# A planned delta-rule and feed-forward kernel: another order of the work, weight decoding moved partly to ScalarE and TensorE, and key tiles of 128 rows

## The chip, the cores and the metric

The kernel runs on one core of one Trainium2 chip. The metric is the device time in microseconds (us); three runs of the kernel before gave 631.62 as their median, from 630.73 to 635.42.

## The reference

Two computations in a row. The first is a delta-rule recurrence for 4 batches x 8 heads over 768 time steps, with a 48 x 48 state per head; the second takes its result as 3072 tokens of 384 channels through a feed-forward layer with 2048 hidden units. The weights come as 64-bit floats.

```python
k_n = k / (np.linalg.norm(k, axis=-1, keepdims=True) + 1e-06)
for t in range(S):
    y[:, :, t] = q_t @ state
    v_old = state^T @ k_n_t
    state = state + beta_t * outer(k_n_t, v_t - v_old)
x = y as (3072, 384)
h = x @ w_in
g = h - np.tanh(h)
out = g @ w_out
```

## The kernel before

**The recurrence** is cut into 24 chunks of 32 steps, and six groups of four chunks. For each chunk `score` (L433) multiplies keys with keys and queries on TensorE, into a bank of PSUM; the key product goes to the group's tile `gs` (`L442` on VectorE for the first four chunks, `L445` on ScalarE for the others), the query product to `pq`, which GpSimd masks. For each group `solve` on VectorE inverts 128 triangular 32 x 32 matrices: a transpose (L476), norms (L485 to L516), a scaling (L519), 30 elimination steps of two instructions each (L530, L532), a second scaling and a transpose into `tt` (L535, L540). Then `chain` goes through the chunks one after the other, since each needs the state that the last one left: keys times state on TensorE (L576, `keyed`), the difference on VectorE (L583, `vsub`), `tt` times values (L608), a copy to SBUF on ScalarE (L614), the new outer products (L622), their addition to the state `st` on VectorE (L648), and the output's two products (L593, L632). `output` transposes a chunk's result (L667) and splits it in a high and a low part, the `xt` tiles (L671 on ScalarE, L673 on VectorE).

**The feed-forward layer** takes the tokens in six blocks of 512 (four chunks each). Every block has 16 units of 128 hidden channels: nine matmuls `ph` (L778), tanh on ScalarE (L795), a subtraction and a high/low split on both engines (L797, L803, L805), and nine matmuls `po` (L828). In the first block the first F0 = 5 units are worked in two halves of 256 tokens, so that they can start after two chunks.

**The weights** are decoded on the chip from the 64-bit words, in 16 pieces of 128 x 768: `c` from the high word on ScalarE (L690), `lo` from the low word on VectorE (L715), both joined on VectorE (L726), the high part `h` cast on ScalarE (L729), and the low part `l = c - h` on VectorE (L744). Each piece serves two units.

**What sets the order.** A planner in the kernel (`Plan.run`) picks the next operation of each engine at build time, from costs, due times and the constants at the end of the file; on the chip each engine then works through its fixed list and waits where a semaphore isn't there yet. While TensorE has nothing to do, the planner puts in padding matmuls on a zero tile (`warm`, L333). `FIRST` is the order of the first loads on SyncE's queue (SP); the weight pieces from AHEAD = 6 on are loaded from ScalarE's queue (`refill`). The tiles of keys and queries (`kc`, `kd`, L341) have KR = 112 rows of 2 x 512 numbers, the two batch pairs at rows 0 to 47 and 64 to 111.

Of the kernel before, what the change touches and what calls it, by code (L numbers as in the profile page):

```python
# [85 lines left out]
class Plan:  # L86
# [3 lines left out]
    SLACK = {"PE": 0.649, "DVE": 0.28, "ACT": 0.098, "POOL": 0.2, "SP": 0.0}  # L90
# [10 lines left out]

    def spawn(self, gen):
        op = next(gen, None)
        if op is not None:
            self.streams.append([gen, op])
# [86 lines left out]
    def run(self):  # L192
        nc, tc = self.nc, self.tc
        code = nc.cur_bb.bb.instructions
        while self.streams:
# [25 lines left out]
            try:  # L221
                item[1] = gen.send((t, end + self.VISIBLE[eng]))
# [24 lines left out]
def kernel(ctx: ExitStack, tc: tile.TileContext, kq, kn, vn, beta, w_in, w_out, const, out):  # L247
# [16 lines left out]
    cs = cst.tile([128, 160], F32, name="cs")  # L264
    ident = cs[:, 0:128]
    strict = cs[:, None, 128:160].broadcast_to([128, H, C])
# [22 lines left out]
    def transfer(end, kb):  # L289
        a = max(dma[0], end + 1.5)  # L290
        dma[0] = a + kb * 1024e-3 / 360.0
        plan.moves.append((a, dma[0]))
        return Event(dma[0] + 0.4)
# [19 lines left out]

    def negate():
        (_, t) = yield Op("ACT", 0.4, (const_in,), 10.0)
        nc.scalar.activation(minus, ident, AF.Copy, scale=-1.0)
        negation.t = t

    def warm():
# [3 lines left out]
        while xt_in[NS - 1].t is None and plan.free["PE"] < 2000.0:  # L323
# [5 lines left out]
            if 0 < len(gram) < 4:  # L329
# [9 lines left out]
    def load_keys(s, table, tag):  # L339
        kc = ld.tile([KR, 2, 16, C], F32, tag=tag, name=f"{tag}{s}", bufs={"kc": KCS, "kd": KDS}[tag])  # L340
# [6 lines left out]
    def load_values(s):  # L347
        v = ld.tile([128, H, D], F32, name="v", bufs=VS)
        nc.sync.dma_start(v, vn[s])
        a = transfer(plan.free["SP"], 192)  # L350
        kt = ld.tile([128, H, D], F32, name="kt", bufs=VS)
        nc.sync.dma_start(kt, kn[s])
        v_of[s] = (v, kt, a, transfer(plan.free["SP"], 192), rv.take())
# [33 lines left out]
    def loads(items):  # L387
        for item in items:
            kind, n = item[0], int(item[1:])
            deps, tag = (), "kd" if kind == "d" or n in (2, 3) else "kc"  # L390
# [6 lines left out]
            yield Op("SP", ISSUE * (2 if kind == "v" else 1), deps=deps, due=when(kind, n))  # L397
            if kind == "k":
                load_keys(n, kc_of, tag)
                if n in (2, 3):  # L400
# [12 lines left out]
    sol = lambda name: at.tile([128, C, C], F32, tag="sol", name=name, bufs=SOLS)  # L413
# [4 lines left out]
    def score(s):  # L418
        g, r = divmod(s, 4)
        deps = (known(kc_of, s, 1),)  # L420
        if r == 0:
            yield Op("PE", 0.0, deps + (rsol, lambda: 0.0 if g < 2 or g - 2 in solved else None), 0.0)
            gs = sol(f"gs{g}")
# [11 lines left out]
        if s not in (2, 3):  # L435
# [4 lines left out]
        if s < 4:  # L440
            (_, t) = yield Op("DVE", dve(256), (scored,), 0.0)
            nc.vector.tensor_copy(to, ps[:, :, 0:C])  # L442
# [17 lines left out]
    def solve(g):  # L460
# [9 lines left out]

        (_, t) = yield V(0, gram_done[g] + [known(beta_of, g, 1), rsol], cost=1.24)
        gs, gsr = groups[g]
        bt, _, btr = beta_of[g]
        a = sol(f"a{g}")
        ar = rsol.take()
        nc.vector.transpose(fl(a), fl(gs))  # L476
        gsr.t = t
# [10 lines left out]
        def triangle():  # L488
            (_, t) = yield Op("POOL", 1.27, (taken,), due(), "lock")
            nc.gpsimd.affine_select(a, a, [[1, C], [-1, C]], ALU.is_gt, 0.0, base=0, channel_multiplier=0)  # L490
# [27 lines left out]
        (_, t) = yield V(C * C, (scaled, tri), mode="lock")  # L518
        nc.vector.scalar_tensor_tensor(a, a, -1.0, gm[:, :, None].broadcast_to([128, C, C]), ALU.mult, ALU.mult)  # L519
# [4 lines left out]
        for j in range(1, C - 1):  # L524
            n = C - 1 - j
            shape = [128, n, j]
            (_, e) = yield V(n * j, (t,), mode="lock")
            tmp = at.tile([128, 240], F32, name="tmp", bufs=2)
            tv = tmp[:, :n * j].rearrange("p (i c) -> p i c", c=j)
            nc.vector.tensor_tensor(tv, a[:, j + 1:, j:j + 1].broadcast_to(shape), a[:, j:j + 1, :j].broadcast_to(shape), ALU.mult)  # L530
            (_, e) = yield V(n * j, (Event(e),), mode="lock")
            nc.vector.tensor_tensor(a[:, j + 1:, :j], a[:, j + 1:, :j], tv, ALU.add)  # L532
            t = Event(e)
        (_, e) = yield V(C * C, (t,), mode="lock")
# [425 lines left out]
```

## Time and profile before

| what | value |
|---|---|
| median of three runs | 631.62 us |
| the profiled execution's own time | 631.85 us |
| its span, first to last instruction | 630.1 us |
| what lies around the span | 1.75 us |
| TensorE busy | 596.3 us, 95% of the span |
| VectorE busy | 396.0 us, 63% |
| ScalarE busy | 203.1 us, 32% |
| GpSimd busy | 46.4 us, 7% |
| padding matmuls (L333) | 164, 46.1 us |
| mean granted TensorE clock | 0.967 |

In the rows of the profile each group has its line, engine, operation, tiles with their shapes, count, busy time and the mean of one; the timeline and the chain of waits give start and duration in us from the span's start; "<-" names what ended an idle time. PE is TensorE's matmuls, PEld its weight loads, DVE is VectorE, ACT ScalarE, POOL GpSimd, SPq and ACTq the DMA issues on SyncE's and ScalarE's queue. A small fp32 matmul has two records.

### The profile page before, as it was taken

To read this page: it belongs to the slowest core of one execution; us is meant where nothing else is said; L and a number is where in the kernel's file an instruction comes from. 1 tells how busy PE (TensorE), PEld (TensorE's weight loads), DVE (VectorE), ACT (ScalarE), POOL (GpSimd) and SP (SyncE) were. 2 spreads that over 40 slices of the span, in tenths; PEclk is the share of its full clock that TensorE was granted. 3 is DMA by queue.
4 is the path that set the end of the run, shared out by engine and by line. 5 is a ranking of instruction groups with operands and counts; after the bars stand their busy time and mean duration, and the time that the engine had idled before them with its cause. 6 is when DMAs were issued, how large, how long until landed. Compare 5 with 4: busy or idle time off the path is not lost.

```text
span 630.1 us, 24015 instructions
## 1 busy us (share of the span) xinstructions
PE 596.3 (95%) x11078; PEld 468.0 (74%) x11078; DVE 396.0 (63%) x853; ACT 203.1 (32%) x365; POOL 46.4 (7%) x60
## 2 busy tenths in 40 slices
PE   6769868999999999999999999999999999999996
PEld 3334547898888878888777888878888878878884
DVE  2859779998889659864278863289863333332331
ACT  2220204575434323224232224332232323332331
POOL 1200301001000010000110000110000000000000
PEclk8779975999999999999999999999999999999998
DMA  9990525361124032122222123022121000010001
GB/s 282 297 316 20 150 84 177 118 212 46 28 57 133 3 96 62 48 69 95 59 74 70 44 57 94 3 57 57 57 91 48 1 3 3 4 51 0 1 0 51
DMA packets 26789, 49.11 MB, mean 78 GB/s; under 512 B 2912, under 2 KB 9184, under 8 KB 26688
## 3 DMA queue, kind: packets, MB, share of 16 engines
q1 hardware_dynamic: 23184, 39.62, 21.2%
q10 hardware_dynamic: 3504, 7.95, 4.0%
q8 instruction: 87, 1.43, 1.0%
q14 instruction: 14, 0.11, 0.1%
HBM read 42.84 MB, written 4.72 MB: 75 GB/s over the span
## 4 chain that ended last, share of the span: by engine, by line
PE 85%; DMA 7%; DVE 5%; issue 1%; ACT 1%; SPq 0%; ACTq 0%
PE po L828 32%; PE ph L778 32%; DMA kc<-in_kq 5%; PE po L333 4%; PE psa L608 3%; PE psa L433 3%; PE psa L622 3%; PE psa L576 3%; PE psy L632 3%; PE psy L593 2%; DMA raw<-in_w_out 2%; PE psa L667 1%; DVE tmp L530 1%; DVE a L532 1%; DVE w L744 1%
## 5 line engine op out<-in xcount | busy, mean ns | idle before, releaser
L828 PE MATMUL po<-gh,w 128*128 128x512 f32 (+1 forms) x909 | 217.6, 388 | 2.3 <-ACT gh L803 2.1
L778 PE MATMUL ph<-xt,w 128*128 128x512 f32 (+1 forms) x909 | 214.9, 386 | 1.7 <-DVE w L744 1.0
L778 PEld LDWEIGHTS ph<-xt,w 128*128 128x128 f32 x909 | 163.5, 189 | 35.9 <-DVE w L744 1.2
L828 PEld LDWEIGHTS po<-gh,w 128*128 128x128 f32 x909 | 162.5, 189 | 36.8 <-ACT gh L803 2.5
L797 DVE TENSOR_TENSOR t<-ph,t 128x512 f32<-128x512 f32 (+1 forms) x101 | 66.9, 664 | 107.5 <-ACT t L795 106.7
L795 ACT ACTIVATE t<-ph 128x512 f32<-128x512 f32 (+1 forms) x101 | 58.2, 577 | 182.0 <-PE ph L778 179.9
L805 DVE TENSOR_TENSOR gh<-t,gh 128x512 fp32r<-128x512 f32 (+1 forms) x101 | 67.0, 664 | 42.5 <-ACT gh L803 41.2
L803 ACT CAST gh<-t 128x512 fp32r<-128x512 f32 (+1 forms) x101 | 60.5, 600 | 68.3 <-DVE t L797 54.6
L532 DVE TENSOR_TENSOR a<-a,tmp 128x30 f32<-128x30 f32 (+9 forms) x180 | 62.7, 348 | 5.4
L530 DVE TENSOR_TENSOR tmp<-a 128x30 f32<-128x30 f32 (+9 forms) x180 | 60.9, 338 | 4.6
L333 PE MATMUL po<-wz 128*128 128x512 bf16 x164 | 46.1, 439 | 3.5 <-issue 2.4
L433 PEld LDWEIGHTS psa<-kc 48*32 48x32 f32 x1408 | 22.3, 112 | 18.8 <-issue 17.4
L333 PEld LDWEIGHTS <-wz 128*128 128x128 bf16 x164 | 16.9, 109 | 26.0 <-issue 12.0
L433 PE MATMUL psa<-kc 48*32 48x64 f32 x1408 | 26.2, 226 | 10.5 <-DMA kc<-in_kq 8.7
L554 POOL TENSOR_TENSOR v<-v,nt 128x384 f32<-128x384 f32 x20 | 18.0, 900 | 225.5 <-DMA v<-in_vn 115.2
L648 DVE TENSOR_TENSOR st<-st,psa 112x384 f32<-112x384 f32 x44 | 22.3, 548 | 15.0 <-PE psa L622 14.5
L445 ACT COPY gs<-psa 128x256 f32<-128x256 f32 x20 | 12.4, 622 | 57.9 <-PE psa L433 57.9
L455 POOL TENSOR_TENSOR pq<-pq,cs 128x256 f32<-128x256 f32 x24 | 19.3, 802 | 147.1 <-ACT pq L449 147.1
L622 PEld LDWEIGHTS psa<-u_sb,kt 32*48 32x48 f32 x1472 | 19.4, 123 | 9.0 <-issue 7.0
L608 PEld LDWEIGHTS psa<-v,tt 32*32 32x32 f32 x1536 | 19.3, 110 | 8.3 <-issue 5.2
L608 PE MATMUL psa<-v,tt 32*32 32x48 f32 x1536 | 22.9, 210 | 1.5 <-issue 1.5
L576 PEld LDWEIGHTS psa<-st,kd 48*32 48x32 f32 x1472 | 18.1, 109 | 7.6 <-issue 5.6
(55 smaller groups left out, 377.9 us busy)
## 6 DMA issues: line engine op xcount, KB each, us to landing
kd<-in_kq SPq DMA_DIRECT2D x23, 448.0 KB, 4.1
kc<-in_kq SPq DMA_DIRECT2D x22, 448.0 KB, 4.4
v<-in_vn SPq DMA_DIRECT2D x24, 192.0 KB, 3.4
kt<-in_kn SPq DMA_DIRECT2D x24, 192.0 KB, 3.4
out<-o SPq DMA_DIRECT2D x18, 256.0 KB, 2.1
raw<-in_w_in ACTq DMA_DIRECT2D x5, 768.0 KB, 6.2
raw<-in_w_out ACTq DMA_DIRECT2D x5, 768.0 KB, 4.9
raw<-in_w_in SPq DMA_DIRECT2D x3, 768.0 KB, 12.0
```

The lines of the kernel that those rows point to most:

```text
L333: nc.tensor.matmul((ps if own else pos[w][0][0]).rearrange("p (a b) -> p a b", a=4), wz, wide, start=own, stop=own, skip_group_check=not own)
L433: nc.tensor.matmul(ps[quad[b], h, :], k[:, 0], k, start=True, stop=True)
L530: nc.vector.tensor_tensor(tv, a[:, j + 1:, j:j + 1].broadcast_to(shape), a[:, j:j + 1, :j].broadcast_to(shape), ALU.mult)
L532: nc.vector.tensor_tensor(a[:, j + 1:, :j], a[:, j + 1:, :j], tv, ALU.add)
L608: nc.tensor.matmul(pu[rows, h, :], tt[rows, 8 * r + h, :], v[rows, h, :], start=True, stop=True)
L622: nc.tensor.matmul(hv(sums[b // 2][0])[HALF[b % 2], h, :], kt[rows, h, :], u_sb[rows, h, :], start=True, stop=True)
L778: nc.tensor.matmul(p, wi[f][:, a, ct, :], xt[:, b, ct, part], start=(ct == 0 and i == 0), stop=(ct == NC - 1 and i == 2))
L795: nc.scalar.activation(t_, p, AF.Tanh)
L797: nc.vector.tensor_tensor(t_, p, t_, ALU.subtract)
L803: nc.scalar.copy(gh[:, 0, :n], t_)
L805: nc.vector.tensor_tensor(gh[:, 1, :n], t_, gh[:, 0, :n].bitcast(F32), ALU.subtract)
L828: nc.tensor.matmul(po[c][:, part], wo[f][:, a, 128 * c:128 * c + 128], gh[:, b, :n], start=(f == 0 and i == 0 and z < 1), stop=(ended.get( ...
```

## The change

Three things are new in what is computed where; the rest is another order.

- **Decoding.** `LOW` is on: `lo` is made by ScalarE from one byte of each low word, instead of by VectorE from the whole word. `SPARE` is 8: for the first eight pieces the low part is made by TensorE, as identity times `c` minus identity times `h` in a bank of PSUM (two halves of 384 columns, an fp32 and an fp32r matmul each), and two copies by ScalarE; VectorE's subtraction stays for the other eight.
- **Loads.** Key and query tiles have 128 rows, 16 of them zeros, instead of 112 (512 KB each instead of 448). Values and natural keys come as one tile of 384 KB instead of two of 192. `FIRST` and the other lists have another order, and only weight pieces 12 to 15 are loaded from ScalarE's queue. The tile of k1 stays in the `kd` buffers as those of k2 and k3 did, so that it isn't loaded a second time.
- **A mask** (`lower`) is multiplied in where VectorE copied the first four chunks' scores.
- **The order.** F0 is 4, the planner's slacks, due times and seed are others, a table `QUIRK` shifts the due time of single operations, and scores from chunk 8 on wait in the planner for chunks of the chain (`LATCH`). `HALVED` is empty and `BURN` is 0, so that the new branches for them issue nothing.

```diff
-    SLACK = {"PE": 0.649, "DVE": 0.28, "ACT": 0.098, "POOL": 0.2, "SP": 0.0}
+    SLACK = {"PE": 0.264, "DVE": 14.746, "ACT": 0.22, "POOL": 0.2, "SP": 0.0}
...
-        kc = ld.tile([KR, 2, 16, C], F32, tag=tag, name=f"{tag}{s}", bufs={"kc": KCS, "kd": KDS}[tag])
+        kc = ld.tile([128, 2, 16, C], F32, tag=tag, name=f"{tag}{s}", bufs={"kc": KCS, "kd": KDS}[tag])
...
-        v = ld.tile([128, H, D], F32, name="v", bufs=VS)
-        nc.sync.dma_start(v, vn[s])
-        a = transfer(plan.free["SP"], 192)
-        kt = ld.tile([128, H, D], F32, name="kt", bufs=VS)
-        nc.sync.dma_start(kt, kn[s])
+        both = ld.tile([128, 2, H, D], F32, name="v", bufs=VS)
+        nc.sync.dma_start(both, vk[s])
...
-            (_, t) = yield Op("DVE", dve(256), (scored,), 0.0)
-            nc.vector.tensor_copy(to, ps[:, :, 0:C])
+            (_, t) = yield Op("DVE", dve(256), (scored, const_in), 0.0)
+            nc.vector.tensor_tensor(to, ps[:, :, 0:C], lower, ALU.mult)
...
-WARM, HOLD, GUARD, F0 = 30.0, 60.0, 0.28, 5
-FIRST = ["k0", "k1", "k2", "k3", "b0", "v0", "w0", "d1", "w1", "v1", "v2", "v3", "b1"]
+WARM, HOLD, GUARD, F0 = 120.0, 150.0, 0.28, 4
+FIRST = ['k0', 'k1', 'k2', 'k3', 'b0', 'v1', 'v3', 'k4', 'w2', 'w4', 'k6', 'w0', 'w3', 'k7', 'v0', 'k5', 'w1', 'v2', 'b1']
-LOW, SPARE = False, 0
-AHEAD, BEHIND = 6, 5
+LOW, SPARE = True, 8
+AHEAD, BEHIND = 12, 3
```

The branch that `SPARE` switches on was in the kernel before:

```python
if i < SPARE:
    for x in (slice(0, DM), slice(DM, 2 * DM)):
        nc.tensor.matmul(ps[:, :DM], ident, c[:, x], start=True, stop=False)
        nc.tensor.matmul(ps[:, :DM], minus, h[:, x], start=False, stop=True)
        nc.scalar.copy(l[:, x], ps[:, :DM])
```

**VectorE, start of the first solve.** The names are tiles: `gs` the scores of the first group, `a` the matrices in work, `lo`, `c` and `w` a piece of weights. Before:

```order
L442 COPY gs_124<-psa_86 128x8x32
L715 TENSOR_SCALAR lo_265<-raw_118 128x768
L726 SCALAR_TENSOR_TENSOR c_263<-c_263,lo_265 128x768
L744 TENSOR_TENSOR w_267<-c_263,w_267 128x768
L442 COPY gs_124<-psa_87 128x8x32
L476 STREAM_TRANSPOSE a_309<-gs_124 128x1024
```

Now:

```order
L465 TENSOR_TENSOR gs_127<-psa_87,cs 128x8x32
L465 TENSOR_TENSOR gs_127<-psa_88,cs 128x8x32
L501 STREAM_TRANSPOSE a_319<-gs_127 128x1024
L511 COPY sq<-a_319 128x32
L529 TENSOR_SCALAR ss<-sq 128x32
```

Three operations of the first weight piece stood ahead of the last copy of scores; now none does. The piece's one remaining operation on VectorE (`c`) comes behind the scaling of `a`, and the transpose of the second group, which stood in the middle of the first solve, comes behind its end.

**TensorE, the third and fourth chunk of the chain**, ahead of the feed-forward layer's first matmuls. `st` is the state, `v,tt` the solved values, `cs,y_sb` a transpose of a result, `xt` the tokens. Before:

```order
L593 MATMUL psy<-st,kd_105 32x48 x32
L608 MATMUL psa_86<-v,tt_711 32x48 x32
L667 MATMUL psa_87<-cs,y_sb 128x128 x3
L667 MATMUL psa_86<-cs,y_sb 128x128 x3
L333 LDWEIGHTS wz
L333 MATMUL po_88<-wz 128x512
L778 MATMUL ph<-xt_1028,w_267 128x256 x9
```

Now, around the second chunk:

```order
L672 MATMUL psa_87<-st,kd_100 32x48 x32
L832 MATMUL ph<-c_593,cs 128x384
L833 MATMUL ph<-w_786,minus 128x384
L832 MATMUL ph<-c_602,cs 128x384
L833 MATMUL ph<-w_847,minus 128x384
L832 MATMUL ph<-c_593,cs 128x384
L833 MATMUL ph<-w_786,minus 128x384
L689 MATMUL psy<-st,kd_100 32x48 x32
L704 MATMUL psa_88<-v,tt_729 32x48 x32
```

The decoding pairs stand between the steps of the chain, where there was padding or nothing. The first `ph` matmuls come behind the keyed products of the third chunk, no longer behind the solved values of the fourth; four half units are done ahead of the fourth chunk's transposes.

**SyncE, the first loads.** Before, to the first weight tile:

```order
L341 DMA kd_105<-in_kq 112x2x512
L360 DMA bt<-in_beta 128x32
L349 DMA v<-in_vn 128x384
L352 DMA kt<-in_kn 128x384
L374 DMA raw_118<-in_w_in 128x3x512
```

Now:

```order
L364 DMA kd_106<-in_kq 128x2x512
L380 DMA bt<-in_beta 128x32
L372 DMA v<-in_vk 128x768 x2
L364 DMA kc_119<-in_kq 128x2x512
L394 DMA raw_123<-in_w_in 128x3x512
L394 DMA raw_160<-in_w_in 128x3x512
L364 DMA kc_162<-in_kq 128x2x512
L394 DMA raw_165<-in_w_in 128x3x512
```

The tile that the first decoded piece needs (`raw_118` before, `raw_165` now) moved behind two other weight tiles, two value tiles and two more key tiles.

198 lines of the change are left out of this document (150 added, 48 removed).

## The prediction

> **What bounds the kernel now.** I read the windows first, to split the span in stages:
>
> ```profile
> 15.00:46.00 31.00, 20.53 (x300) 10.30 (x299) 21.75 (x56) 7.42 (x14) 4.80 (x7) 0.78 1.03 308
> 61.00:104.00 43.00, 33.54 (x1311) 23.96 (x1300) 33.65 (x88) 10.02 (x21) 7.21 (x9) 0.81 0.42 121
> 104.00:124.00 20.00, 18.29 (x409) 16.05 (x410) 19.11 (x36) 9.32 (x20) 2.03 (x2) 0.90 0.51 151
> 124.00:624.00 500.00, 497.00 (x8711) 403.70 (x8710) 303.15 (x635) 172.39 (x307) 29.50 (x35) 1.00 0.17 51
> ```
>
> The columns are PE, PEld, DVE, ACT and POOL busy, the granted clock, the DMA share and GB/s. From 124 us on TensorE works without a gap at full clock (497.0 of 500 us): there only less work on TensorE shortens the kernel. Ahead of 124 us it waits and pads, and what counts is how early the feed-forward layer can start. So the chain of waits and the timelines of the start come next. TensorE:
>
> ```profile
> 13.58 1.49 PE L433 MATMUL psa<-kd 48*32 48x64 f32 x45 [3.45 <-issue]
> 15.01 5.65 PE L333 MATMUL po<-wz 128*128 128x512 bf16 x16
> 63.38 0.88 PE L608 MATMUL psa<-v,tt 32*32 32x48 f32 x64
> 125.71 0.88 PE L608 MATMUL psa<-v,tt 32*32 32x48 f32 x64
> ```
>
> The fourth chunk's scores end at 15.1 us (after 3.45 us of "issue", which is neither engine nor load). The chain's first `tt` product stands at 63.4 us, that of chunk 4 at 125.7. VectorE:
>
> ```profile
> 14.66 0.56 DVE L715 TENSOR_SCALAR lo<-raw 128x768 int32<-128x768 int32 x1 [4.73 <-DMA raw<-in_w_in]
> 18.35 0.61 DVE L442 COPY gs<-psa 128x256 f32<-128x256 f32 x1
> 18.99 1.25 DVE L476 STREAM_TRANSPOSE a<-gs 128x1024 f32<-128x1024 f32 x1
> 25.25 1.22 DVE L519 SCALAR_TENSOR_TENSOR a<-a,gm 128x1024 f32<-128x1024 f32 x1
> 45.51 1.25 DVE L476 STREAM_TRANSPOSE a<-gs 128x1024 f32<-128x1024 f32 x1 [6.28 <-ACT gs L445]
> 60.67 0.53 DVE L554 TENSOR_TENSOR v<-v,nt 128x384 f32<-128x384 f32 x1
> ```
>
> The first solve is the path from 19 to 61 us, and it loses time twice to its place in VectorE's list: its last scores wait behind a weight piece that landed at 14.66 us, and in its middle stands the second group's transpose, 6.28 us early. From 61 us on the chain of four chunks runs among the second solve's steps; VectorE is busy for 33.65 of 43 us, then 19.11 of 20, and TensorE waits for its results.
>
> **The change part by part.** *Start of the solve.* With nothing ahead of it the last copy of scores (0.61) follows the scores at 15.1, so the transpose starts at 15.8 us, 3.2 earlier. The new mask makes a two-operand instruction of four copies; I cost it at nothing, the span from copy to transpose being the same 0.61 (a second operand from SBUF; at worst 0.3 us in all, from the 0.61 of the one that is last).
>
> *The solve.* From 18.99 to the end of the first value scaling, 60.67 + 0.53 = 61.2, are 42.2 us. Out of them go 6.28 of waiting, 1.25 of the second transpose and 0.53 of another chunk's scaling: 34.1. Two joins of weight pieces come in:
>
> ```profile
> L726 DVE SCALAR_TENSOR_TENSOR c<-c,lo 128x768 int32<-128x768 int32 x16 | 15.2, 949 | 0.5 <-ACT c L690 0.4
> L744 DVE TENSOR_TENSOR w<-c,w 128x768 fp32r<-128x768 f32 x16 | 15.8, 988 | 1.0 <-ACT w L729 0.9
> L715 DVE TENSOR_SCALAR lo<-raw 128x768 int32<-128x768 int32 x16 | 9.3, 579 | 4.8 <-DMA raw<-in_w_in 4.7
> L690 ACT ACTIVATE c<-raw 128x768 f32<-128x768 f32 x16 | 14.4, 908 | 9.2 <-DMA raw<-in_w_in 4.3 <-DVE w L744 4.0 <-DMA raw<-in_w_out 0.8
> L729 ACT CAST w<-c 128x768 fp32r<-128x768 f32 x16 | 13.3, 833 | 11.9 <-DVE c L726 11.9
> L797 DVE TENSOR_TENSOR t<-ph,t 128x256 f32<-128x256 f32 x10 | 4.0, 417 | 0.1
> L614 ACT COPY u_sb<-psa 128x384 f32<-128x384 f32 x24 | 11.5, 479 | 31.8 <-PE psa L608 22.6 <-DVE tmp L530 9.1
> ```
>
> That is 34.1 + 2 x 0.95 = 36.0, so VectorE has the values ready at 15.8 + 36.0 = 51.8 us, if the first join doesn't wait.
>
> *The loads.* The join is reached some 7 us into the solve (before, L519 stood 25.25 - 18.99 = 6.3 behind the transpose and took 1.22), at 23.3 us. Its weight tile is now behind about 6.4 MB: six key tiles of 0.52, two value tiles of 0.39, three weight tiles of 0.79. The DMA rate differs by what moves:
>
> ```profile
> 0.80 0.89 SPq L341 DMA_DIRECT2D kc<-in_kq  x2
> 18.21 1.39 SPq L341 DMA_DIRECT2D kc<-in_kq  x3
> 20.00:26.00 6.00, 1.70 (x69) 1.07 (x66) 5.42 (x20) 0.00 (x0) 1.44 (x2) 1.00 1.05 246
> 28.00:35.00 7.00, 5.22 (x124) 3.05 (x114) 6.31 (x19) 2.44 (x6) 1.63 (x2) 0.74 1.04 389
> ```
>
> Behind the three key tiles issued from 18.21 us on, the window from 20 us holds key tiles; the later one holds mostly weights: 246 against 389 GB/s, the engines full in both. With the first issue at 0.80 us I let the bytes flow from 2 us on (an estimate). At 389 the tile is there at 2 + 16.5 = 18.5 us, and with two ScalarE operations of 0.91 the join can start at 20.3: no wait. With the key tiles still at 246 it would be 2 + 3.1/0.246 + 3.3/0.389 = 23.1 and 24.9: 2 us late, and less than the 3 us by which TensorE's list is later anyway, below. So the rows price the 128 rows between nothing and 14% more bytes in the shadow of the solve; I take nothing. [...] In the steady part neither matters: the DMA share is 0.17. The values' two issues become one, and ScalarE's queue loses six weight issues to SP's, which are in the list ahead of the chain's later loads; the weights land before the chain starts, so nothing there is late by it.
>
> *TensorE's list ahead of the chain.* Between the fourth chunk's scores and the first `tt` product stand 141 padding matmuls, four scores and two decode pairs:
>
> ```profile
> 44.83 15.81 PE po L333 x69
> 42.94 1.89 PE psa L433 x64
> 60.65 1.03 PE psa L433 x64
> 143.93 0.86 PE psa L622 x64
> 213.66 2.04 PE po L828 x9
> 133.27 1.08 PE po L828 x9
> 220.81 2.29 PE po L828 x9
> 73.25 0.55 PE L667 MATMUL psa<-cs,y_sb 128*128 128x128 f32 x3 [0.60 <-ACT y_sb L657]
> ```
>
> Padding is 15.81/69 = 0.229 each, 141 x 0.229 = 32.3; scores 4 x 1.03 = 4.1; a start at lower clock costs what the 16 after 15.01 us took more, 5.65 - 3.7 = 2.0. No fp32 matmul of 128 rows is in the trace. The scores run 8 of 64 columns one behind another in 1.03 us, 2.0 ns a column, which makes 0.77 for 384; the transposes, 0.55 for 3 x 128, make 0.55 as the lower end. I take 0.64, and 0.17 for the fp32r one (2.04/9 x 384/512): 0.81 a pair, 1.6 for two. Sum: 15.1 + 32.3 + 4.1 + 2.0 + 1.6 = 55.1 us. TensorE's own padding, not VectorE, ends last: the chain starts at **55.1** instead of 63.4, 8.3 earlier.
>
> *Four chunks.* From there to the second half of the first units stand on TensorE 18 chain products (0.86: 15.5), four transposes (0.55: 2.2), 12 decode pairs (9.7), 72 half-width matmuls (1.08/9: 8.6), 21 paddings (4.8) and some 14 changes from small to large matmuls (2.29 - 2.04: 3.5): 44.3 us. VectorE, busy 33.65 us in the old stretch, loses `lo` and `l` of three pieces (0.58 + 0.99 each), gets two more joins (1.9) and the gates of four more half units (two of 0.42 each, 3.4): some 34. ScalarE has six `lo` and seven `c` (0.91), five casts (0.83), 13 low-part copies and 12 copies of the chain (0.48), 28 us, and some 3 of gates. So the stretch is TensorE's, and I add 4 us of waits where a step needs a result at once (the old stretch shows TensorE idle for 43 - 33.54 = 9.5): 55 + 48 = **103 us**.
>
> *From there to the end.* Before, 125.71 to the last product, 622.91 + 0.91 = 623.82, are 498.1 us:
>
> ```profile
> 622.91 0.91 PE po L828 x2
> 624.45 2.02 DMA out<-o
> ```
>
> Against that point the new list at 103 us still has five more scores (5.2), two more keyed products (1.7), two more half units (2.2) and the seventh decoded piece's two pairs (1.6), less 0.2 by F0 = 4: 10.5 us. End: 103 + 498.1 + 10.5 = 611.6, 12.2 us earlier.
>
> *One tight place.* The third group's scores now stand 17 groups of nine matmuls (34.7) and three chunks' products (some 15) ahead of the product that needs its `tt`: 50 us.
>
> ```profile
> L532 DVE TENSOR_TENSOR a<-a,tmp 128x30 f32<-128x30 f32 (+9 forms) x180 | 62.7, 348 | 5.4
> L530 DVE TENSOR_TENSOR tmp<-a 128x30 f32<-128x30 f32 (+9 forms) x180 | 60.9, 338 | 4.6
> L797 DVE TENSOR_TENSOR t<-ph,t 128x512 f32<-128x512 f32 (+1 forms) x101 | 66.9, 664 | 107.5 <-ACT t L795 106.7
> ```
>
> VectorE's list holds between them the elimination, (62.7 + 60.9)/6 = 20.6, some 10 for the solve's rest, seven units at 1.33 and three chunks at 2.2: 46.5, with small ones some 48. With the copy ahead of it and waits within, that product comes 2 us late (0 to 6): 613.6, 10.2 earlier. The profiled time is 631.85, 0.2 above the median of the runs: 631.85 - 10.2 = **621.6 us**.
>
> **Rivals.** (1) *More.* If the 3.45 us of "issue" shrink with faster loads, the four chunks take 1 us of waits instead of 4, and the tight place none: 621.6 - 3.4 - 3 - 2 = 613. For it: sums on VectorE and ScalarE leave room. Against: "issue" waits are all over the start. (2) *The cold clock eats it.* The clock was 0.81 from 61 to 104 us; were it so again, 44.3 us would be 44.3/0.81 = 54.7 in place of 48.3, and the time 621.6 + 6.4 = 628. [...] Against: pairs and half units now fill the gaps that made the clock fall. (3) *Slower: ScalarE's list becomes the chain's limit.* Twelve copies of the chain (`u_sb`, `y_sb`, `xt`) stand among `c`, `lo`, casts and low-part copies. Should each wait for two of 0.91, that is 12 x 1.82 = 21.8, less the 4 counted: 621.6 + 17.8 = 639. It turns the sign from 10.2 + 4 = 14.2 us, 1.2 us for each copy. For it: ScalarE's work there goes from 10.02 to some 31 us, in fixed order. Against: 31 of 48 leaves room. (4) *The 128 rows don't speed the loads up.* 14% more bytes and the 2 us at the join stay behind TensorE's padding: 622, inside the forecast.
>
> **How the numbers follow.** Forecast, (4) included: 0.48, 617 to 627. (1) 0.15, (2) 0.26, (3) 0.11. A measurement of this kernel can tell about 1% from no change, that is 625.3 and 637.9. Faster: (1) and nearly all of the forecast, 0.61, and 0.02 of (2): 0.63. Within 1%: the rest of the forecast and of (2), and the milder part of (3): 0.28. Slower: 0.09. Range: from the middle of (1), 612, to beyond (2), 633.
>
> **What would show it.** Right: the first transpose of VectorE at 15.8 us, no wait within the first solve, the first `tt` product at 55, full work on TensorE from about 103, the last product near 613. Wrong: the join of the first piece waiting for its load, padding that runs on well beyond 55 us, idle times of TensorE behind `u_sb` or `xt` on ScalarE, a clock under 0.9 from 60 to 100 us, or a wait of over 6 us for the third `tt`.

## The result, and the profile after

The changed kernel takes **622.77 us** (median; 621.83 to 624.19) against 632.03 for the kernel before on the same chip: the ratio is 0.985, with a 95% interval of 0.980 to 0.989. The forecast was 621.6 us. Its profiled execution took 623.54 us with a span of 621.8.

The windows of the changed kernel, in the order of those shown of the kernel before (PE, PEld, DVE, ACT and POOL busy, granted clock, DMA share, GB/s):

```profile
15.00:46.00 31.00, 31.00 (x367) 15.72 (x367) 28.58 (x75) 10.33 (x18) 5.04 (x7) 0.92 1.04 388
55.00:103.00 48.00, 46.96 (x1278) 36.72 (x1277) 36.32 (x98) 28.41 (x55) 5.91 (x6) 1.00 0.27 86
103.00:124.00 21.00, 21.00 (x284) 17.38 (x283) 18.57 (x35) 13.67 (x22) 0.00 (x0) 1.00 0.20 64
124.00:616.00 492.00, 483.00 (x8824) 390.08 (x8823) 282.31 (x597) 163.81 (x293) 32.95 (x40) 0.99 0.19 57
```

The front is better than before: 388 GB/s in place of 308 at first, then TensorE busy for 46.96 of 48 us and at full clock, where it had been busy for 33.54 of 43 at 0.81. The last row is worse: 9.0 of 492 us idle, where it had been 3 of 500. So there are two stories, a gain ahead of 100 us and a loss behind it. The start on VectorE, from its timeline:

```profile
15.62 1.25 DVE L501 STREAM_TRANSPOSE a<-gs 128x1024 f32<-128x1024 f32 x1
23.50 0.95 DVE L823 SCALAR_TENSOR_TENSOR c<-c,lo 128x768 int32<-128x768 int32 x1
51.85 1.93 DVE L650 TENSOR_TENSOR v<-v,nt 128x384 f32<-128x384 f32 x4
```

The transpose comes 3.4 us earlier than before, the join of the first piece of weights stands there without a wait in brackets, and the first of the four value scalings is done near 52.4 us. TensorE, from its timeline:

```profile
13.36 1.50 PE L456 MATMUL psa<-kd 48*32 48x64 f32 x47 [3.44 <-issue]
44.73 9.23 PE L356 MATMUL po<-wz 128*128 128x512 bf16 x42
53.89 0.88 PE L704 MATMUL psa<-v,tt 32*32 32x48 f32 x64
96.50 3.74 PE L875 MATMUL ph<-xt,w 128*128 128x256 f32 x25
134.22 0.88 PE L704 MATMUL psa<-v,tt 32*32 32x48 f32 x64
135.03 0.96 PE L875 MATMUL ph<-xt,w 128*128 128x512 f32 x3
138.69 3.92 PE L875 MATMUL ph<-xt,w 128*128 128x512 f32 x10 [2.70 <-issue]
194.65 1.65 PE L875 MATMUL ph<-xt,w 128*128 128x512 f32 x6 [1.95 <-DVE t L894]
322.65 0.36 PE L689 MATMUL psy<-st,kd 48*32 48x48 f32 x11 [1.57 <-issue]
415.60 1.42 PE L925 MATMUL po<-gh,w 128*128 128x512 f32 x5 [1.22 <-issue]
614.64 2.11 PE L925 MATMUL po<-gh,w 128*128 128x512 f32 x8 [0.23 <-DVE gh L902]
```

Padding runs up to the chain's first product at 53.9 us (63.4 before), and the second half of the first units is reached at 96.5. Behind it come three waits put down to "issue", that is, to no engine and no load that the profile names. With a smaller one (0.53 us, at 188) they make 6.0 us; the kernel before has none behind 124 us. The bracket of the first row is the same wait as in the kernel before (3.45 us): it became neither shorter nor longer, with loads at 344 GB/s from 2 to 8 us in place of 292.

After the two longest waits the clock goes down as well (windows of the same run):

```profile
138.00:140.00 2.00, 1.31 (x5) 1.04 (x5) 0.00 (x0) 0.00 (x0) 0.00 (x0) 0.83 0.08 20
140.00:142.00 2.00, 2.00 (x7) 1.51 (x6) 0.42 (x1) 1.05 (x2) 0.00 (x0) 0.50 0.00 0
142.00:144.00 2.00, 2.00 (x19) 1.40 (x21) 0.96 (x2) 1.00 (x3) 0.00 (x0) 0.82 0.00 0
322.00:324.00 2.00, 1.35 (x15) 1.09 (x15) 1.88 (x4) 0.00 (x0) 1.26 (x1) 0.91 0.44 166
324.00:326.00 2.00, 2.00 (x7) 1.52 (x6) 1.54 (x8) 0.00 (x0) 0.00 (x0) 0.50 0.90 230
326.00:328.00 2.00, 2.00 (x8) 1.64 (x7) 0.00 (x0) 0.00 (x0) 0.00 (x0) 0.74 0.12 44
```

What the lower clock costs I estimate from these windows, as busy time times what is missing to 1: 1.31 x 0.17 + 2 x 0.50 + 2 x 0.18 = 1.6 us behind the first wait, and 0.12 + 1.0 + 0.52 = 1.6 behind the other. Together 6.0 + 3.2 = 9.2 us went behind 97 us that the forecast did not have.

### The profile page after: what moved, and what is told of

The parts are those of the page before. It is cut to its first block, busy times and chain, and to the rows that moved or that the text cites. A ratio compares the mean times of both kernels' runs of the same rounds, so it can differ in the third digit from the quotient of the medians.

```text
span 621.8 us, 24085 instructions
## 1 busy us (share of the span) xinstructions
PE 602.0 (97%) x11120; PEld 470.8 (76%) x11120; DVE 378.5 (61%) x827; ACT 221.5 (36%) x396; POOL 46.3 (7%) x60
## 3 DMA queue, kind: packets, MB, share of 16 engines
q8 instruction: 87, 1.43, 0.9%
## 4 chain that ended last, share of the span: by engine, by line
PE 94%; DVE 2%; issue 2%; ACT 1%; DMA 0%; ACTq 0%; DVEq 0%
PE ph L875 33%; PE po L925 32%; PE po L356 7%; PE psa L456 4%; PE psa L719 3%; PE psa L704 3%; PE psy L729 3%; PE psa L672 3%; PE psy L689 2%; PE ph L832 2%; PE psa L764 1%; DVE a L579 1%; DVE tmp L577 1%; PE ph L833 0%; DMA out<-o 0%
## 5 line engine op out<-in xcount | busy, mean ns | idle before, releaser
L875 PE MATMUL ph<-xt,w 128*128 128x512 f32 (+1 forms) x900 | 217.1, 390 | 5.3 <-issue 2.7
L579 DVE TENSOR_TENSOR a<-a,tmp 128x30 f32<-128x30 f32 (+9 forms) x180 | 61.0, 339 | 4.7
L356 PE MATMUL po<-wz 128*128 128x512 bf16 x176 | 44.8, 407 | 1.1 <-DVE idle L315 1.1
L456 PEld LDWEIGHTS psa<-kc 48*32 48x32 f32 x1344 | 20.4, 110 | 7.1 <-issue 6.5
L719 PEld LDWEIGHTS psa<-u_sb,v 32*48 32x48 f32 x1472 | 18.8, 120 | 9.2 <-issue 7.9
L456 PE MATMUL psa<-kc 48*32 48x64 f32 x1344 | 23.9, 222 | 0.0
L754 ACT COPY y_sb<-psy 128x384 f32<-128x384 f32 x24 | 11.5, 479 | 34.3 <-PE psy L729 34.3
L770 DVE TENSOR_TENSOR xt<-psa,xt 128x384 fp32r<-128x384 f32 x24 | 13.3, 555 | 16.1 <-ACT xt L768 16.1
L704 PEld LDWEIGHTS psa<-v,tt 32*32 32x32 f32 x1536 | 17.9, 105 | 6.3 <-issue 2.8
L719 PE MATMUL psa<-u_sb,v 32*48 32x48 f32 x1472 | 21.7, 205 | 1.0 <-issue 1.0
```

What stands on the lines that cost most here:

```text
L356: nc.tensor.matmul((ps if own else pos[w][0][0]).rearrange("p (a b) -> p a b", a=4), wz, wide, start=own, stop=own, skip_group_check=not own)
L456: nc.tensor.matmul(ps[quad[b], h, :], k[:, 0], k, start=True, stop=True)
L579: nc.vector.tensor_tensor(below, below, tv, ALU.add)
L704: nc.tensor.matmul(pu[rows, h, :], tt[rows, 8 * r + h, :], v[rows, h, :], start=True, stop=True)
L719: nc.tensor.matmul(hv(sums[b // 2][0])[HALF[b % 2], h, :], kt[rows, h, :], u_sb[rows, h, :], start=True, stop=True)
L875: nc.tensor.matmul(p, wi[f][:, a, ct, :], xt[:, b, ct, part], start=(ct == 0 and i == 0), stop=(ct == NC - 1 and i == 2))
```

## The experiments

The questions: what did the 128 rows bring, what did the decoding on ScalarE and TensorE bring, and what are the waits for "issue"? All ratios are to the kernel before on the same chip as the run; its median differs from chip to chip (631.7 to 633.1 us), so small differences between rows are better read from the ratios.

| kernel | median us | ratio (95%) | "issue" behind 97 us |
|---|---|---|---|
| changed kernel | 622.77 | 0.985 (0.980 to 0.989) | 6.0 |
| 112 rows | 624.34 | 0.988 (0.985 to 0.991) | 5.4 |
| kernel before with 128 rows | 627.12 | 0.993 (0.991 to 0.995) | 0 |
| `lo` on VectorE | 619.83 | 0.980 (0.977 to 0.983) | 4.2 |
| low part on VectorE | 617.74 | 0.978 (0.975 to 0.981) | 2.5 |
| both on VectorE | 619.77 | 0.981 (0.979 to 0.983) | 1.7 |
| 96 pads less | 627.21 | 0.992 (0.990 to 0.995) | 4.8 |
| 6 pads less | 618.17 | 0.978 (0.975 to 0.980) | 5.0 |
| more loads | 622.17 | 0.985 (0.983 to 0.987) | 5.4 |
| heavy loads | 647.99 | 1.025 (1.021 to 1.029) | 13 |
| no late key loads | 621.51 | 0.983 (0.980 to 0.986) | 4.2 |
| four kd buffers | 623.69 | 0.987 (0.985 to 0.989) | 6.2 |
| 24 pads less | **616.89** | 0.974 (0.972 to 0.976) | 1.65 |

**The rows, in the changed kernel.**

```diff
-        kc = ld.tile([128, 2, 16, C], F32, tag=tag, ...)
+        kc = ld.tile([KR, 2, 16, C], F32, tag=tag, ...)
-    kq = np.zeros((NS, 2, 128, 16, C), np.float32)
+    kq = np.zeros((NS, 2, KR, 16, C), np.float32)
```

> The changed kernel with the key tiles and their layout in DRAM at 112 rows again; all else as in the changed kernel. Main theory (the rows only matter to the transfers of the front, which padding covers there): the key tiles fall from the 388 GB/s of 15 to 46 us towards the 246 GB/s that they had before, the weights and keys of the front land up to about 4 us later, and VectorE waits for the later keys again, but TensorE's list ahead of the chain ends at 53.9 us and VectorE's values were ready at 52.4, so at most 2 to 3 us come through: 623 to 626 us. Rival (the rows carry the gain): 630 us or more. Rival (the rows are worth nothing to the transfers): the rate stays at 388 GB/s and the time at 622.8.

Windows of the changed kernel, and of this one, in which nearly nothing but key tiles moves:

```profile
2.00:8.00 6.00, 6.00 (x135) 2.97 (x137) 1.20 (x3) 0.60 (x3) 0.00 (x0) 1.00 1.00 344
8.00:14.00 6.00, 2.31 (x126) 2.03 (x118) 1.27 (x3) 1.12 (x3) 2.18 (x3) 0.92 1.05 387
```

```profile
2.00:8.00 6.00, 5.85 (x127) 2.93 (x129) 1.25 (x3) 0.75 (x4) 0.00 (x0) 1.00 1.01 266
8.00:14.00 6.00, 1.91 (x108) 1.54 (x97) 1.20 (x2) 0.96 (x3) 2.17 (x3) 0.88 1.05 311
```

The last column is the point: 344 against 266 GB/s at the same DMA share of 1.0, so the rows do set the rate here. What it does to the first scores, in TensorE's timeline with 112 rows:

```profile
8.94 1.10 PE L456 MATMUL psa<-kd 48*32 48x64 f32 x64 [0.56 <-DMA kd<-in_kq]
10.57 0.44 PE L456 MATMUL psa<-kd 48*32 48x64 f32 x17 [0.54 <-DMA kd<-in_kq]
14.38 1.50 PE L456 MATMUL psa<-kd 48*32 48x64 f32 x47 [3.37 <-issue]
```

The scores wait for key tiles, and the last of them come at 14.38 instead of 13.36 us. With the 16 rows of zeros a key tile comes faster: 344 x 112/128 = 301 GB/s without the zeros, against 266. Why, no run shows. With 112 rows the chain's first product stands at 55.55 instead of 53.89 us, and the median is 1.6 us higher. The intervals of the two ratios overlap, and the profiled execution of this kernel, the fastest of its six, even ended 0.35 us ahead of that of the changed kernel: after its wait of 2.49 us at 139.71 the clock stayed at 1.00 (0.991 over the whole run, against 0.988). So what is shown is a delay of 1.7 us at the chain's start; the 1.6 us at the end agree with it but are not clear of the noise. The main theory holds in size, with the place corrected: 1.0 us of the delay enters at the first scores, not at the join, and padding doesn't cover it, since it stands behind the scores in TensorE's list and shifts with them.

**The rows, in the kernel before.** The same edit the other way round.

> The kernel before with the 128-row key tiles and layout alone. Main theory (with VectorE's chain of decoding ahead of the first values, faster loads only take away part of its wait): the transfers of the front go from some 250 to some 390 GB/s, the wait of VectorE of 6.28 us for a key tile at 45.5 us shrinks by up to 4 us, and the time falls to 627 to 630 us from 632.0. Rival (the wait for loads is all that the change took away): 623 us. Rival (the loads are covered by something else): 632.

627.12 us, where the kernel before took 631.72 on the same chip: 4.6 less, or half of the change's gain, by the rows alone. VectorE's wait for the late key tile, 6.28 us before, in this run's timeline:

```profile
41.09 1.25 DVE L476 STREAM_TRANSPOSE a<-gs 128x1024 f32<-128x1024 f32 x1 [2.90 <-ACT gs L445]
```

The rows are worth 4.6 us where VectorE waits for loads and some 1.6 where its list has been rearranged so that it doesn't. The two gains of the change (rows, order) overlap.

**The decoding.** Three kernels give `lo`, the low part, or both back to VectorE, in the changed kernel's order.

```diff
-            nc.scalar.activation(lo, lw, AF.Copy, scale=7.49 / 255.0)
+            nc.vector.tensor_scalar(lo, raws[i].rearrange("p (n b) -> p n b", b=2)[:, :, 0], 29, None, ALU.logical_shift_right)
```

```diff
-                nc.tensor.matmul(ps[:, :DM], ident, c[:, x], start=True, stop=False)
-                nc.tensor.matmul(ps[:, :DM], minus, h[:, x], start=False, stop=True)
-                nc.scalar.copy(l[:, x], ps[:, :DM])
+                nc.vector.tensor_tensor(l[:, x], c[:, x], h[:, x].bitcast(F32), ALU.subtract)
```

> The changed kernel with lo made by VectorE's shift again and not by ScalarE; the low part stays on TensorE. Theory (neither engine limits behind 97 us, and ahead of it padding covers VectorE up to 1.5 us): VectorE pays 0.6 us for each of the pieces in the front, so its first values come 2 to 4 us later than 52.4, the chain's first product 1 to 3 us later than 53.9: 623.5 to 626 us. Rival (ScalarE's lo is what a later piece waits for): under 622 us.

> The changed kernel with the low part of decoded weights taken by VectorE (a subtraction of each half) in place of the two products on TensorE and ScalarE's copy; lo stays on ScalarE. Theory (behind the chain's start TensorE is what is full, 98% of the time; a pair of products costs 0.82 us): 16 pairs are 13 us of TensorE, of which those ahead of the chain stand where padding ends last and count too, so 610 to 614 us if VectorE (61% busy) takes 16 times 0.6 us without a wait. Rival (the pairs stand in time in which TensorE would wait for VectorE anyway, or VectorE's place in the chain is tight): 621 to 626 us, with new waits of TensorE for VectorE.

> The changed kernel with lo and the low part both by VectorE, so with the decoding that the kernel before has (in the order of the changed kernel), and its 128-row key tiles. Theory (what the decoding on ScalarE and TensorE gave is VectorE's time ahead of the chain's start, and it costs TensorE 13 us that count behind it): VectorE's first values come 5 to 8 us later than 52.4, the chain's first product at 57 to 60, and TensorE gets 13 us back: 612 to 620 us. Rival (the new decoding carries the gain): 628 to 632 us, as VectorE's list delays the start and waits take what TensorE is given.

The fifth chunk's product behind `tt` stands, in the changed kernel, at 134.22 us; with `lo` on VectorE at 134.36, with the low part there at 134.17, with both at 137.50. So either relief of VectorE is enough for the whole 3.3 us, and the second brings nothing. The expectation for `lo` had the wrong sign; its rival has the number but not the reason, since nothing comes earlier at 134 us. The one for the low part was half right. The pairs did not cost 13 us: 14 of the 16 stand ahead of 94 us, and without them TensorE waits in their place for ScalarE (TensorE's waits from 55 to 97 us, low part on VectorE):

```profile
PE psy L689 <- ACT y_sb L754: 2.8, 1, 2.8
PE psa L764 <- ACT y_sb L754: 2.1, 2, 1.5
```

The run with both on VectorE lies within the range expected of it, but not for the reason given: its chain starts at 53.95 us, not at 57 to 60.

All three kernels end earlier than the changed kernel, although none is ahead of it by over 0.05 us at 134 us. The difference lies in the waits behind, here at 136 us with `lo` on VectorE:

```profile
136.88 3.61 PE L875 MATMUL ph<-xt,w 128*128 128x512 f32 x15 [0.75 <-issue]
```

0.75 us in place of 2.70, and no lower clock after it (15 products take 3.61 us here, where 10 took 3.92): 3.5 us of this kernel's gain fall between 134 and 168 us. The run with both edits is 3.3 us behind at 134 us and 2.6 ahead at the end.

**The clock.** The 96 paddings from 24 to 54 us are left out, by the edit that is shown for the next kernel, with other numbers.

> The changed kernel without all 96 padding products in the stretch from about 24 to 54 us (no part of the result). Theory (they hold the clock): TensorE idles in 24 to 52 us but for the pairs of decoding, the granted clock in 55 to 100 us falls from 1.00 to 0.55 to 0.8 as it was in the kernel before, and the time rises by 5 to 12 us to 628 to 635 us. Rival (the clock comes back at once with the work): the chain starts 1.5 us earlier and the time is 621 us.

627.21 us, 4.4 more than the changed kernel and just under what was expected. The mechanism is smaller than expected:

```profile
52.00:56.00 4.00, 4.00 (x111) 2.82 (x115) 3.44 (x6) 2.00 (x4) 1.32 (x1) 0.53 0.02 4
56.00:60.00 4.00, 4.00 (x172) 2.66 (x161) 2.85 (x10) 3.50 (x6) 0.60 (x1) 1.00 0.36 102
```

The clock is 0.53 for the first 4 us of work and then at 1.00 (1.00 in the windows from 56 to 80 us too). By these windows the cold start costs 4 x 0.47 = 1.9 us, an estimate, not ten. These windows are from the fastest of the six executions (624.61 us); what makes the others up to 4.5 us longer stays open.

**Fewer pads at the end of the padding.**

```diff
+            pads[0] += 1
+            if 148 <= pads[0] <= 153:
+                continue
```

> The changed kernel without the last 6 of the padding products ahead of the chain's first product (padding is no part of the result). Theory (padding ends last there: VectorE had its first values at 52.4 us, TensorE came to the product that takes tt at 53.9): the product starts at 52.5, 1.4 us earlier, and the time falls by as much, to 621.4 us. Rival (TensorE is no longer what ends last there, VectorE is): the product stays at 53.9 us and the time at 622.8. The waits of TensorE that the profile puts down to nothing (6.0 us together behind 97 us) stay where they are if they follow from the shape of the work; if they follow from the place of the instructions in memory they move, since everything behind lies 12 instructions earlier.

The chain starts at 52.52 us, 1.4 earlier, so padding did end last. But the time fell by 4.6 us, not 1.4, and the waits for "issue" changed their places. Counted through TensorE's program (a small fp32 product is two matmuls in the records), they lie, to within a few matmuls, at these numbers (96 pads less has one more, the long wait ahead of the chain's first product, which is no border):

- changed kernel: 221, 1880, 2647, 3923, 6475, 8260
- 6 pads less: 221, 2647, 3157, 3540, 3923, 4816, 6475
- low part on VectorE: 221, 1881, 2519, 3157, 5708, 8643
- 96 pads less: 221, 1115, 1625, 2519, 6347, 7113, 7496, 8134
- kernel before: 221, 476, 1240, 1496, 1624, 1752, 1880

All are 221 plus a multiple of about 127.6, whatever stands there: 3923 - 221 = 29 x 127.7, 6475 - 221 = 49 x 127.6, 8134 - 221 = 62 x 127.6. At 2647 the changed kernel has done three products of a group of nine (135.03 us in its timeline, the wait follows); with 6 pads less:

```profile
132.47 2.34 PE L880 MATMUL ph<-xt,w 128*128 128x512 f32 x9
135.94 1.29 PE L880 MATMUL ph<-xt,w 128*128 128x512 f32 x5 [1.12 <-issue]
```

All nine are done here before the wait: it has stayed at the same number of the program, and the work has moved by six. The profile has a queue that fits (DMA queues of the changed kernel: packets, MB, share):

```profile
q8 instruction: 87, 1.43, 0.9%
```

1.43 MB in 87 packets are 16.4 KB each, and the program has 11,120 matmuls, 127.8 for each packet. I read these packets as TensorE's program, which then comes over the DMA engines in pieces of some 128 matmuls with their weight loads (the trace has 11,120 of each). The waits at the borders are up to 3.45 us long, and behind 97 us each ends 1.2 to 1.6 us after such a packet has landed, as is shown below.

**What makes a border cost something: loads or density?** Three kernels change the loads: a further 256 KB beside each late key load; six of them (the edit shown); and no late key loads at all.

```diff
+        if s > 7 or (tag == "kd" and s > 3):
+            for i in range(6):
+                nc.sync.dma_start(junk[i % 3], kq[s, 0].rearrange("p u c -> p (u c)"))
```

> The changed kernel with a further load of 256 KB beside each late key load (into a tile that nothing reads), so that more is under way on the DMA queues from about 130 us on. Theory A (the waits of TensorE that the profile puts down to nothing, 2.70 us at 136, 1.57 at 321 and 1.22 at 414 us, come from dense stretches of small products whose instructions can't be supplied in time): they stay within 1 us, 622.8 to 624 us. Theory B (transfers in flight hold up the supply of instructions): they grow to 10 us or more in all, and the time to 627 us or more.

> The changed kernel with six further loads of 256 KB behind each of the 36 late loads of key tiles, on the same queue, into tiles that nothing reads; the computing engines' instructions are the same in the same order. The DMA share goes from 0.19 to about 0.45 behind 100 us. Theory C (the next 16 KB of TensorE's program queue behind transfers): the waits for nothing grow from 6.0 us behind 97 us to 12 us or more, and the time to 628 us or more. Theory A (the supply has its own pace): within 2 us of 622.8, but for a wait for a key tile that comes late, which the profile would name as DMA.

> The changed kernel without the 36 late loads of key tiles (the late chunks use the early tiles again, so that part of the input is left out); the instructions of the four computing engines are the same in the same order. Every wait of TensorE for nothing lies, in all runs so far, at a fixed place of its program, some 127.6 matmuls from the one before or a multiple of that, and the profile has an instruction queue on the DMA engines with packets of 16 KB, 87 of them for 11,120 matmuls. Theory C (the next 16 KB of TensorE's program queue behind a key tile on the same DMA engines): the waits of 2.70, 0.53, 1.57 and 1.22 us shrink to a fraction, the lower clock after them goes with them, and the time falls by 4 to 8 us to 615 to 619 us. Theory A (the dense stretches use up the instructions faster than they can come at all): they stay, 621 to 623 us.

TensorE's waits behind 97 us, with heavy loads and then without late key loads:

```profile
PE ph L880 <- DVE t L899: 8.1, 1, 8.1
PE psy L694 <- issue: 5.4, 4, 2.7
PE psy L734 <- issue: 3.1, 3, 1.8
PE ph L880 <- issue: 1.6, 1, 1.6
```

```profile
PE ph L879 <- issue: 2.1, 1, 2.1
PE psy L693 <- issue: 2.1, 2, 1.5
PE ph L879 <- DVE t L898: 1.9, 1, 1.9
```

Without the late key loads 4.2 us are left of 6.0: only the wait at 415 us is gone. (Its four runs took 619.5, 619.9, 623.2 and 623.3 us, so the median says little here.) So the key loads are not the main cause. Loads of values and weights go on in that run, and no run leaves those out. With 57 MB more the waits for "issue" more than double, to 13 us, at more borders, as theory C said of this run: this many transfers do hold the program up. (Of the rest of the 25 us there, some 6 are a longer wait for one `t`, 8.1 us in place of 1.9, for which VectorE had itself waited 5.4 us for ScalarE.) One further load each changes nothing (5.4 us of "issue").

**An earlier start of the key loads.** `bufs={"kc": KCS, "kd": KDS + 1}[tag]`, nothing else.

> The changed kernel with four buffers in place of three for the second load of key tiles; nothing else. A load into three buffers can start only when the chain has used the oldest, which is the end of a dense stretch of small products, and so just when TensorE needs the next piece of its program; with four it starts a chunk earlier. Theory C (program behind loads): the waits at 136 and 414 us, each behind a load issued there, shrink; 2 to 5 us less, 618 to 621 us, unless the earlier loads meet another dense stretch. Theory A: 622.8 us.

623.69 us, and 6.2 us of "issue" in place of 6.0: no effect. The key loads are not what holds these borders up.

**Density.** The other suspect is how fast TensorE works off a piece of its program: 128 big matmuls take some 29 us (9 take 2.04 in the rows of before), 128 small ones 1.8 (64 in 0.88). In the order of the changed kernel three places have 192 small matmuls in a row (three groups of 64, as the keyed, `yk` and `tt` products ahead of 134.22 + 0.88 us), from the matmuls 2452, 6294 and 8066 on; the longest waits stand at 2647, 6475 and 8260, each a border at which nearly all of the 128 matmuls just done belong to such a run. The kernel before has one such place behind 124 us, and 704 small matmuls in a row from 82.5 us on, in which the last four of its waits lie. So the suspicion is that the next piece isn't there yet where a whole piece lies within such a run. That can be tried by shifting the borders alone:

```diff
+            if 130 <= pads[0] <= 153:
+                continue
```

> The changed kernel without the last 24 padding products ahead of the chain's first product (no part of the result), 18 more than in the run with 6 less. In all runs so far TensorE's waits for nothing lie at its 221st matmul and multiples of some 127.6 behind it, where the next 16 KB of its program begin. Worked out from the durations of the single products, each such piece (128 matmuls with their weight loads) that TensorE works off in under 3 us is short of supply by the rest; with 24 products fewer ahead, the borders fall such that these shortages behind the fourth chunk sum to 0.8 us in place of 4.9. Theory (place of the borders decides): the chain starts at 52.5 us as with 6 less, the waits for nothing behind 97 us fall from 6.0 us to 2 or less, the clock stays at 1.00 from 124 us on, and the time is 613 to 616.5 us, the fastest of all. Rival (density or loads decide, not the borders): waits of 5 to 6 us as before, 618 to 621 us. A 4 us gap of TensorE ahead of the chain may cost up to 1 us by a lower clock in both.

TensorE's timeline in this run:

```profile
51.79 0.88 PE L709 MATMUL psa<-v,tt 32*32 32x48 f32 x64 [3.66 <-issue]
171.35 0.45 PE L694 MATMUL psy<-st,kd 48*32 48x48 f32 x21 [0.93 <-issue]
190.08 3.73 PE L880 MATMUL ph<-xt,w 128*128 128x512 f32 x9 [2.82 <-DVE t L899]
233.61 0.36 PE L734 MATMUL psy<-u_sb,pq 32*32 32x48 f32 x11 [0.72 <-issue]
```

Two waits for "issue", 1.65 us, are left behind 97 us, and the window from 124 to 190 us has a clock of 1.00. Behind 190 us the expectation fails in part: the wait for VectorE's `t` is 2.82 us here (1.95 in the changed kernel), and the clock is 0.61 over the next 4 us (nine products take 3.73). The median of 616.89 us is the lowest of all, 5.9 under the changed kernel, 0.4 above the expected range on a chip on which the kernel before took 633.1. The chain's start gained 2.1 us, less some 1.4 by the clock (0.64 in its first 4 us); the rest are the borders, less what is lost at 190 us. That their place decides is shown, with 1.65 us of waits in place of 6.0; the rival falls.

**The packets themselves.** The trace keeps the start and the duration of each of the 87 packets, and with them the two causes can be told apart. Over all fourteen profiles here, TensorE has 56 waits for "issue" behind 97 us; each lies at a border, and each ends 1.2 to 1.6 us after the packet of the next piece has landed. In the changed kernel a packet starts 0.8 us (median) after TensorE has passed the border before and takes 1.0. Together with 1.4 us behind its landing that makes some 3.2 us for a piece, an estimate from these three. So there are two ways to wait:

- *A short piece.* Ahead of the waits at 321 and 414 us the piece was worked off in 1.60 and 2.62 us, with no load under way ahead of the packet. This is the part that density explains.
- *A late packet.* At 136 us the packet starts 2.97 us after the border. The border was passed at 133.32 us, the packets of a 768 KB weight load on ScalarE's queue start from 133.57 to 136.36, and the program's packet starts at 136.29. With `lo` on VectorE the border is passed at 133.32 as well, but that load starts at 134.15 and only a few of its packets are ahead of the program's, which starts at 134.44: the wait is 0.75 us in place of 2.70. The two waits left with 24 pads less are of this kind too: pieces of 4.2 and 4.1 us, packets 2.3 and 2.4 us after the border, with 0.4 and 0.5 MB of loads under way.

So theory C was wrong about the key tiles, but not about loads. That the weight and value loads delay the packet is read from the order of packets in these traces; no run takes those loads away.

## Why the prediction was right, step by step

*Right, and for the reason given:* the first transpose (15.8 forecast, 15.6 measured), the solve without a wait (values at 51.8 and 52.4), the join (23.3 and 23.5), the padding that ends last (taking 6 pads away brought the chain's start forward by as much), the full clock from 60 to 100 us (1.00, so rival 2 falls; in the kernel before it had been 0.50 from 81 to 84 us, behind a wait of 2.44), and ScalarE with its work in the order of the chain but no limit to it (28.4 of 48 us; rival 3 falls). Also the tight place: 2 us forecast, 1.95 measured, because VectorE's list is full with the third solve. The wait stands at a `t` of the feed-forward layer, 12 us ahead of the product named, which itself (207.13 us) doesn't wait; that the two numbers are so close is luck. Rival 4's premise falls (the 128 rows do speed the loads up, 344 GB/s against 266), although its time lay inside the forecast.

*The terms that were mis-sized.* (a) TensorE's list ahead of the chain: 53.9 instead of 55.1. The padding's 0.229 us each came at a lower clock, 0.95 over those 15.81 us; the last 42 took 9.23 us at 1.00, 0.220 each, which makes 1.3 for 141. (b) "I add 4 us of waits" and the 44.3 us of work for the four chunks: together 42.6 were enough in place of 48.3, with one wait of 0.96. The decoding pairs that the sum charged to TensorE take the place of waits for ScalarE, as the kernel without them showed. The prediction also read the old stretch wrongly: it took TensorE's 9.5 us of idle time from 61 to 104 us for waits for VectorE's results, but 6.9 of them were "issue". In the kernel before:

```profile
PE po L333 <- issue: 2.4, 1, 2.4
PE psa L576 <- issue: 2.0, 1, 2.0
PE psa L608 <- issue: 1.5, 1, 1.5
PE psy L593 <- issue: 0.7, 1, 0.7
PE psy L632 <- issue: 0.3, 1, 0.3
```

These are borders too (1240, 1496, 1624, 1752 and 1880 in the list above), and the two longest waits followed pieces of 1.55 and 2.15 us of work. With pairs and half units among the small products, the pieces of the new order from 55 to 97 us take 2.75 us and more, all but one of them 3.7 or more: a part of the gain at the front is that TensorE waits for "issue" there for 0.96 us only, in place of 6.9.

*Mis-sized as well:* (c) "I take nothing" for the 128 rows: no row of before shows a key tile of that size, so 389 GB/s for it was the prediction's estimate, and the runs showed 344 from 2 to 8 us. Against the same kernel with 112 they are worth some 1.6 us. The sum didn't miss them by that, since it took the end of the first scores from the kernel before (15.1 us, now 14.9), where the new order of loads with 112 rows would have brought them 1 us later.

*The step that failed:* "Before, 125.71 to the last product ... are 498.1 us", carried over to the new order with the added work alone. From 96.5 us, where the second half of the first units begins, to the first of the last eight products at 614.64 the changed kernel took 518.1 us; by the sum it would have been 509.7 (from 103 to 612.7, which is the 613.6 less the 0.91 of the last row). The 8.4 us more are the 9.2 of waits at borders of the program with the lower clock after them, less 0.8 of other terms (among them a wait of 2.12 us for `gh` near the end of the kernel before, which is gone). The profile of before gave the sign: the wait of 3.45 us at 13.58 us and its like up to 101 us were "issue" with no reason known, and the prediction counted on them in one rival only, as something to shrink. The two errors, 6.5 us too late at the units and 8.4 too little behind them, nearly cancel: 1.9 us are left, and the profiled execution took 623.54 against 621.6. The total was closer than its terms, and that is luck.

*What the change's two new computations are worth.* The rows alone bring 4.6 us of the 9.3. The rest, by subtraction, comes with the order; no run tried the order alone. `lo` on ScalarE or the low part on TensorE bring 3.3 us at the chain's fifth chunk, either of them; both together bring no more, and in this kernel less than they cost, because of where the borders fall in it.

*What stays open.* No run takes away the weight and value loads that stand ahead of the late packets. Counting what a piece lacks to some 3 us, an estimate from these runs, chose the better place of the borders, but knows nothing of late packets and so misses single waits (0.8 us expected, 1.65 measured). And the clock doesn't fall after each long wait: it did after 1.57 us, and not after the 2.49 us with 112 rows.

## What to carry to other kernels

When an engine works without a gap in one order, its next order need not: look for runs of small instructions that are longer than one piece of its program (192 against 128 here), for large loads that start just where the next piece is due, and for "issue" waits at equal distances in instructions (127.6 matmuls here), before carrying a busy stretch over. A few paddings more or less ahead of such a stretch shift all the borders behind them (6 fewer moved the work at 2647 by six matmuls), so variants that differ by 1% are to be compared by their waits, not by their medians alone. Rows of zeros that bring a tile from 112 to 128 rows can be worth more than the bytes they add (301 GB/s of data against 266 here), but count the gain only where something waits for that load (4.6 us in the kernel before, some 1.6 in the changed one).

## What the runs showed of the hardware

- The instruction queue q8 moved 87 packets of 16.4 KB over the DMA engines for this kernel, read here as TensorE's program. Behind 97 us, all of TensorE's 56 waits for "issue" in these fourteen profiles lie at their borders, 127.6 matmuls apart: 0.2 to 2.7 us, more of them with 57 MB of further loads (13 us against 6.0). TensorE went on 1.2 to 1.6 us after the packet had landed; a piece worked off in 1.60 us was followed by a wait of 1.57.
- After a wait of 1.57 or 2.70 us the granted clock stood at 0.50 in a window of 2 us and cost another 1.6 us each, by estimate; after 1.22 us it stayed at 1.00, and so it did after 2.49 us with 112 rows; behind a wait of 0.75 us with `lo` on VectorE 15 products took 3.61 us, where 10 took 3.92 behind the one of 2.70. So a wait of 1.57 us was followed by the lower clock, and a longer one was not.
- Without the 96 paddings TensorE was busy for 8.22 us from 24 to 50 and 0.07 from 50 to 52; the clock was 0.53 for the next 4 us and then 1.00.
- Key tiles of 112 rows moved at 266 GB/s and of 128 rows at 344 (301 without the zeros), at a DMA share of 1.01 and 1.00.
